# A second staging set for expert weights, with loads, squares and sums a stage apart

## The chip, the cores and the metric

The kernel runs on one core of a Trainium2 chip. Its engines are TensorE (PE, and PEld for its weight loads), VectorE (DVE), ScalarE (ACT), GpSimd (POOL) and SyncE (SP), which here only issues DMAs. The metric is the device time of one execution in microseconds; lower is better.

## What is computed

Three blocks follow each other:

```python
# 1. attention in chunks of 64 tokens, 4 x 8 heads, 576 tokens, head size 64
attn = softmax(q_c @ k_c.T / 8); x = attn @ v_c          # x: 2304 x 512
# 2. mixture of 8 experts, each token to its best one
e = argmax(x @ w_gate); gate_w = softmax(x @ w_gate)[e]
h = relu(disp[e] @ w1[e])                                # w1[e]: 512 x 1024
out[i] = gate_w[i] * (h @ w2[e])                         # w2[e]: 1024 x 512
# 3. feed-forward
hh = out @ w_in; y = (hh * sigmoid(hh)) @ w_out          # w_in: 512 x 2048
```

The capacity of an expert is 576 tokens. The weights of the feed-forward come as 64-bit floats.

## The kernel before

Matrix products are done in pairs of 16-bit numbers: a matrix is scaled by a power of two, rounded to 16 bits (the high half), and the remainder is the low half; three products of halves make one product. The scale of a weight matrix comes from the sum of its squares.

The expert phase has one stage for each expert e. In a stage the kernel runs `moe_tile(e, 0)`, then `more(e, 1)`: nested `If`s that run further tiles j = 1, 2, ... while the expert has more than 128 j tokens. A tile is 128 tokens: gathered from `x_d` (`gather`, GpSimd), transposed by a DMA (`t_dma`, SP), multiplied by w1 (L845), passed through Relu (`hh` on ScalarE, the low half `hl` on VectorE), multiplied by w2 (L866), scaled, split and scattered to `y_d` (GpSimd). The two halves of the first layer have a PSUM tile each.

Beside this the stage prepares the weights of the next experts. Weights of one expert are 8 pieces of 512 KB, 4 of w1 (m = 0) and 4 of w2 (m = 1). `w_prep(e, m, ...)` returns five steps: `sq(c)` squares piece c on ScalarE and sums each partition, `red` adds over partitions on TensorE (`total`, L124), `sc` reads that on VectorE and makes the scale, `hi(c)` makes the high half on GpSimd, `lo(c)` the low half on VectorE. The pieces lie in `st_s`, one set of 8; when `lo(c)` of expert e + 1 has read a piece, `lo_ld` issues the load of the same piece of expert e + 2 into its place, on SP's queue. Also in the stage, two chunks of `w_in` are converted from 64 bits by three VectorE operations each (`cb`) and squared on ScalarE (`cn`, L808).

The order on every engine is written out by hand. `slots[0]` to `slots[4]` hold what is issued at five places of `moe_tile(e, 0)`: before the first half, after it, after the second half, the same place again, and at three quarters of the second layer. `arms[j]` has the same for tile j inside the `If`. For j = 1 the `Else` arm runs `arms[0]`; for greater j it runs what is left of `arms[j]` and after. Each engine works through its own instructions in this order, and SP issues its DMAs in it.

In the stage of e the kernel before squares w2 of e + 1 (slots 1 and 2), sums and scales it (slot 4), makes the halves of e + 1, and, in `arms[1]` or the `Else` arm, squares, sums and scales w1 of e + 2, which has been loaded in the same stage. `win` and `wot` are regions for the converted weights of the feed-forward; in the expert phase conversions write `win` alone, and `wot` (17 rows of 512 floats in each partition) is first written after it.

In the profiled execution the 20 tiles are, by expert, 4, 1, 4, 3, 2, 1, 3 and 2.

Of the kernel before, what the change touches and what calls it, by code (L numbers as in the profile page):

```python
# [22 lines left out]
def attention_moe_ffn_kernel(  # L23
# [15 lines left out]
    nc = tc.nc  # L39
    B, H, S, D = q.shape  # L40
    NT, DM = out.shape
    E = w_gate.shape[1]
# [24 lines left out]
    st_s = [[(stage0, stage)[m].tile([P, 1024], F32, name=f"st{m}{c}") for c in range(4)] for m in range(2)]  # L67
# [32 lines left out]
    def pow2(n2, s, inv, kf, e2):  # L100
        n2i = n2.bitcast(I32)
        nc.vector.tensor_scalar(e2, n2i, 24, None, ALU.logical_shift_right)
        nc.vector.tensor_scalar(s.bitcast(I32), e2, -EXP1, kf * EXP1, ALU.mult, ALU.add)
        nc.vector.tensor_scalar(inv.bitcast(I32), e2, EXP1, (254 - kf) * EXP1, ALU.mult, ALU.add)  # L104
# [15 lines left out]
    def sums(m, n):  # L120
        return sum_at[-1][:, 16 * m:16 * m + n]

    def total(m, part):
        nc.tensor.matmul(out=sums(m, part.shape[-1]), lhsT=ones32, rhs=part)  # L124
# [3 lines left out]
    w_sp = {}  # L128
    w_fac = {}

    def w_piece(e, m, c):
        t = st_s[m][c]
        if m == 0:
            nc.sync.dma_start(out=t, in_=w1[e, c * P:(c + 1) * P, :])
        else:
            nc.sync.dma_start(
                out=t.rearrange("p (k f) -> p k f", k=2),
                in_=w2[e, 2 * c * P:(2 * c + 2) * P, :].rearrange("(k p) f -> p k f", p=P),
            )

    def w_load(e, m):
        for c in range(4):
            w_piece(e, m, c)

    def w_prep(e, m, hi_eng, lo_eng):
        st = st_s[m]
        sp = []
        n2 = wsm.tile([P, 4], F32, tag=f"n2{m}", name="n2", bufs=2)
        t2 = wsm.tile([P, 1], F32, tag=f"t2{m}", name="t2", bufs=2)
        e2 = wsm.tile([P, 1], I32, tag=f"e2{m}", name="e2", bufs=2)  # L150
        s = wsm.tile([P, 1], F32, tag=f"s{m}", name="s")
        inv = wsm.tile([P, 1], F32, tag=f"i{m}", name="inv")
        w_sp[e, m] = sp
        w_fac[e, m] = inv

        def sq(c):
            nc.scalar.activation(out=junk, in_=st[c], func=ACTF.Square, accum_out=n2[:, c:c + 1])  # L157

        def red():
            total(m, n2)  # L160

        def sc():
            nc.vector.tensor_reduce(out=t2, in_=sums(m, 4), axis=AX, op=ALU.add)
            pow2(t2, s, inv, KW, e2)

        def hi(c, hi_eng=hi_eng):
            if c == 0:
                sp.extend(ring.tile([P, 2, 1024], F16, tag=f"w{m}{i}", name="wsp") for i in range(4))
            if hi_eng is nc.scalar:
                nc.scalar.activation(out=sp[c][:, 0, :], in_=st[c], func=ACTF.Copy, scale=s)  # L170
            else:
                hi_eng.tensor_scalar(sp[c][:, 0, :], st[c], s, 1.0, ALU.mult, ALU.mult)  # L172

        def lo(c):
            lo_eng.scalar_tensor_tensor(  # L175
                out=sp[c][:, 1, :], in0=st[c], scalar=s, in1=sp[c][:, 0, :], op0=ALU.mult, op1=ALU.subtract
            )

        return sq, red, sc, hi, lo
# [116 lines left out]
    part = acc_p.tile([P, 1], F32, name="part")  # L296
# [276 lines left out]
    for t in range(-3, NTILE):  # L573
# [19 lines left out]
        u, i = divmod(t + 3, 2)  # L593
# [41 lines left out]
    prep = {(1, m): w_prep(1, m, nc.gpsimd, nc.vector) for m in range(2)}  # L635
# [29 lines left out]
    r = NBT - 1  # L665
# [43 lines left out]
    reg_p = tc_pool("reg", 1, reuse_waits="tile")  # L709
    win = reg_p.tile([P, KFF + 1, 512], F32, name="win")  # L710
    wot = reg_p.tile([P, KFF + 1, 512], F32, name="wot")
    fn2 = reg_p.tile([P, 2, KFF], F32, name="fn2")
    ft2 = reg_p.tile([P, 2], F32, name="ft2")
    fe2 = reg_p.tile([P, 2], I32, name="fe2")
# [175 lines left out]
    def g_next(e, j):  # L890
        gather(e, j, tabs[:, 0, e, j:j + 1])
# [89 lines left out]
    for e in range(E):  # L981
        last = e + 1 == E
        ops = [f_conv(c) for c in conv_of[e]]
        cb, cn = [lambda o=o: [f() for f in o[0:3]] for o in ops], [o[3] for o in ops]
        slots = [[], [], [], [], []]
        if not last:
            _, _, _, hi1, lo1 = prep[e + 1, 0]
            sq2, red2, sc2, hi2, lo2 = prep[e + 1, 1]

            def lo_ld(m, c):  # L990
                (lo1, lo2)[m](c)
                if e + 2 < E:
                    w_piece(e + 2, m, c)

            l1s, l2s = [[lambda m=m, c=c: lo_ld(m, c) for c in range(4)] for m in range(2)]
            g2 = lambda: g_next(e, 2)
            slots[0] = [lambda: g_next(e + 1, 0), *[lambda c=c: hi1(c) for c in range(4)]] if e else []
            slots[1] = [l1s[0], lambda: sq2(0), lambda: sq2(1)]
            slots[2] = [lambda: sq2(2), lambda: sq2(3), l1s[1], l1s[2], l1s[3]]
            slots[3] = [*([g2] if e else []), lambda: g_next(e + 1, 1)]  # L1000
            slots[4] = [red2, sc2, *[lambda c=c: hi2(c) for c in range(4)]]
        else:
            sp = [lambda c=c: f_split(0, c) for c in range(NSP)]
            slots = [[*cb, *cn], [], [], [], [lambda: f_red(0), lambda: f_sc(0), *sp]]

        def nxt0(k):
            if k < 0:
                if 0 < e < E - 1:
                    t_dma(e, 1)
            elif k == 0:  # L1010
                t_f1(e, 1)
                if last:
                    g_next(e, 2)
                else:
                    t_dma(e + 1, 0)
            elif not last:
                t_f1(e + 1, 0)
            else:
                with tc.If(n_e[e] <= SPLIT0):
                    y0_fac()  # L1020

        if e + 2 < E:
            for m in range(2):
                prep[e + 2, m] = w_prep(e + 2, m, nc.gpsimd, nc.vector)
        moe_tile(e, 0, *cols(e, 0), nxt0, lambda k: [f() for f in slots[k]])

        arms = {j: [[], [], [], [], []] for j in range(NJ)}
        if not last:
            sqs, red, sc = [], [], []
            if e + 2 < E:  # L1030
                sq, r, c1, _, _ = prep[e + 2, 0]
                sqs, red, sc = [lambda c=c: sq(c) for c in range(4)], [r], [c1]
            arms[0] = [*l2s, *sqs, *red, *cb, *cn, *sc]
            arms[1] = [l2s[0:1], [l2s[1], *sqs[0:2]], [*l2s[2:4], *sqs[2:4], cb[0], cn[0]], [], [*red, *sc]]
            arms[2] = [[], cb[1:2], [*cb[2:], *cn[1:]], [], []]
        else:
            arms[0] = []
        more(e, 1, arms)
        if e + 2 == E:
            t_dma(E - 1, 1)  # L1040
            with tc.If(n_e[E - 1] <= SPLIT0):
                y0_load()
# [122 lines left out]
    while conv:  # L1165
        step, left = [], left + 1.5
        c = NSP + len(bg)
# [29 lines left out]
    for s in range(len(seq) + LAG):  # L1197
        if s < len(seq):
            b, f = seq[s]
# [10 lines left out]
        if s >= LAG:  # L1210
            b, f = seq[s - LAG]
# [43 lines left out]
```

## Time and profile before

| what | value |
|---|---|
| median of 3 runs | 853.31 us (850.73 to 855.67) |
| profiled execution, its own time | 850.38 us |
| its span, first to last instruction | 848.6 us |
| busy: PE, PEld | 722.5 us (85%), 440.5 us (52%) |
| busy: DVE, ACT, POOL | 448.1, 333.2, 359.4 us |
| mean granted TensorE clock | 0.929 of full speed |
| weight pieces of the experts | 64 DMAs of 512 KB, 6.4 us to landing (median) |

Busy time is an average over phases with different limits. Attention lasts to about 150 us, the experts from there to 437 us, and the feed-forward to the end.

### The profile page before, as it was taken

The page shows a single profiled execution, that of the slowest core. Times are in us where ns is not written, and L with a number is a line of the kernel's source. Part 1 is how long each engine was busy: PE and PEld are TensorE (multiplying, and loading weights), DVE is VectorE, ACT ScalarE, POOL GpSimd, SP SyncE. Part 2 cuts the span into 40 slices and gives each one's busy share as a digit, 9 for nine tenths or more (in the row PEclk, how much of TensorE's full clock was granted, in tenths as well). Part 3 has the DMA queues.
Part 4 walks back from the last instruction along what each step waited for, and adds up shares of the span by engine and source line. Part 5 has one row for each costly group of instructions (what it writes and reads, how often), then busy time and mean ns, then how long its engine had stood idle before and what let it go on. Part 6 is the DMA issues. An engine that isn't in the chain of part 4 may idle for free.

```text
span 848.6 us, 14692 instructions
## 1 busy us (share of the span) xinstructions
PE 722.5 (85%) x5526; PEld 440.5 (52%) x5526; DVE 448.1 (53%) x920; ACT 333.2 (39%) x615; POOL 359.4 (42%) x355
## 2 busy tenths in 40 slices
PE   4798764998489989569798776999999999999995
PEld 3677654765456756447553333444444444565442
DVE  4365886654794758678339999633322223222000
ACT  5586737443443536442134455322232223223010
POOL 3475632524571737665167535544223223212111
PEclk9797955899699999979899999999999999999999
DMA  7988983992986798895635235020001000001000
GB/s 170 230 231 206 191 239 59 306 273 56 303 246 162 177 235 239 241 237 123 135 72 102 73 125 124 1 51 1 1 37 38 1 1 37 14 1 39 13 37 38
DMA packets 133325, 103.20 MB, mean 122 GB/s; under 512 B 85472, under 2 KB 112096, under 8 KB 133216
## 3 DMA queue, kind: packets, MB, share of 16 engines
q1 hardware_dynamic: 126784, 83.41, 40.2%
q0 software_dynamic: 5760, 18.39, 7.3%
q8 instruction: 60, 0.98, 0.5%
q14 instruction: 49, 0.40, 0.2%
q10 hardware_dynamic: 672, 0.02, 0.0%
HBM read 73.45 MB, written 14.71 MB: 104 GB/s over the span
## 4 chain that ended last, share of the span: by engine, by line
PE 30%; DVE 8%; issue 7%; DMA 4%; POOL 2%; ACT 1%; POOLq 0%; ACTq 0%; DVEq 0%
PE ops L1143 14%; PE fh L1115 14%; DMA out_dram<-ob,yrow 3%; DVE g L1126 2%; DVE th L1121 2%; DVE wot L797 1%; DVE wot L802 1%; PE mh L845 1%; DVE wot L794 1%; DVE win L734 1%; DMA y_d<-yr,tabs 1%; PE myp L866 0%; POOL win L751 0%; POOL win L749 0%; POOL win L750 0%
## 5 line engine op out<-in xcount | busy, mean ns | idle before, releaser
L1143 PE MATMUL ops<-wot,gh 128*128 128x512 f16 x576 | 171.3, 379 | 0.0
L1115 PE MATMUL fh<-yT,win 128*128 128x512 f16 (+1 forms) x768 | 156.9, 355 | 7.0 <-DVE g L1126 7.0
L1130 POOL TENSOR_TENSOR gl<-g,gh 128x512 f16<-128x512 f32 (+1 forms) x80 | 91.9, 1151 | 163.8 <-ACT gh L1128 163.8
L1115 PEld LDWEIGHTS <-win 128*128 128x128 f16 x960 | 94.2, 98 | 118.1 <-issue 26.1
L845 PE MATMUL mh<-mxT,wsp 128*128 128x128 f16 x1920 | 125.6, 233 | 17.7 <-PEq L930 9.4
L845 PEld LDWEIGHTS <-wsp 128*128 128x128 f16 x1920 | 123.5, 106 | 24.1 <-issue 19.9
L1143 PE MATMUL ops<-wot,gl 128*128 128x512 f16 x288 | 109.2, 379 | 0.0
L1121 DVE TENSOR_TENSOR th<-fh,rb 128x512 f32<-128x512 f32 (+1 forms) x64 | 39.8, 622 | 130.7 <-PE fh L1115 130.7
L1122 ACT ACTIVATE th<-th,fi 128x512 f32<-128x512 f32 (+1 forms) x80 | 54.3, 679 | 133.8 <-DVE th L1121 132.9
L175 DVE SCALAR_TENSOR_TENSOR wsp<-st,s,wsp 128x1024 f16<-128x1024 f32 x64 | 99.6, 1591 | 6.0 <-POOL wsp L172 6.0
L866 PE MATMUL myp<-wsp,hh 128*128 128x512 f16 x320 | 96.5, 384 | 0.0
L1143 PEld LDWEIGHTS <-gh 128*128 128x128 f16 x576 | 56.4, 98 | 64.1
L172 POOL TENSOR_SCALAR wsp<-st,s 128x1024 f16<-128x1024 f32 x56 | 75.2, 1359 | 20.0 <-DVE inv L104 11.4
L1128 ACT CAST gh<-g 128x512 f16<-128x512 f32 (+1 forms) x80 | 45.9, 574 | 73.2 <-DVE g L1126 54.3
L157 ACT ACTIVATE junk<-st 128x1024 bf16<-128x1024 f32 x64 | 67.4, 1053 | 16.4 <-DMA st<-in_moe_w_dram 15.3
L1126 DVE TENSOR_TENSOR g<-fh,th 128x512 f32<-128x512 f32 (+1 forms) x80 | 50.7, 634 | 38.8 <-ACT th L1122 32.4
L866 PE MATMUL myp<-wsp,hl 128*128 128x512 f16 x160 | 61.6, 385 | 8.2 <-DVE hl L851 8.0
L819 POOL DMA_INDIRECT xg<-x_d,tabs x34 | 45.4, 1336 | 35.2 <-issue 9.5
L882 POOL DMA_INDIRECT y_d<-yr,tabs x20 | 23.5, 1175 | 79.3 <-DVE yr L879 36.8
L851 DVE SCALAR_TENSOR_TENSOR hl<-mh,hh 128x512 f16<-128x512 f32 x40 | 27.5, 687 | 48.3 <-ACT hh L850 48.3
L1115 PE MATMUL fh<-st,win 128*128 128x512 f16 x192 | 43.5, 379 | 10.6 <-DVE g L1126 9.3
L866 PEld LDWEIGHTS <-hh 128*128 128x128 f16 x320 | 30.7, 101 | 29.8 <-ACT hh L850 0.8
(194 smaller groups left out, 849.8 us busy)
## 6 DMA issues: line engine op xcount, KB each, us to landing
st<-in_moe_w_dram SPq DMA_DIRECT2D x64, 512.0 KB, 6.4
fs<-in_moe_w_in_dram SPq DMA_DIRECT2D x16, 512.0 KB, 7.0
fs<-in_moe_w_out_dram SPq DMA_DIRECT2D x16, 512.0 KB, 3.4
vbd<-in_v_dram SPq DMA_DIRECT2D x72, 64.0 KB, 3.4
x_d<-xr SPq DMA_DIRECT2D x9, 512.0 KB, 6.1
ku<-in_k_dram SPq DMA_DIRECT2D x6, 512.0 KB, 5.7
qu<-in_q_dram SPq DMA_DIRECT2D x6, 512.0 KB, 8.3
ku<-in_k_dram SPq DMA_DIRECT2D x2, 384.0 KB, 4.2
```

The lines of the kernel that those rows point to most:

```text
L157: nc.scalar.activation(out=junk, in_=st[c], func=ACTF.Square, accum_out=n2[:, c:c + 1])
L172: hi_eng.tensor_scalar(sp[c][:, 0, :], st[c], s, 1.0, ALU.mult, ALU.mult)
L175: lo_eng.scalar_tensor_tensor(out=sp[c][:, 1, :], in0=st[c], scalar=s, in1=sp[c][:, 0, :], op0=ALU.mult, op1=ALU.subtract)
L845: nc.tensor.matmul(out=ps[:, f4, :], lhsT=a[c][:, part, f0:f0 + P], rhs=xt[:, rc, :], start=(n == 0), stop=(n == 3 * KD - 1),)
L866: nc.tensor.matmul(out=yp, lhsT=lh[:, f % 4, :], rhs=b[f // 2][:, part, (f % 2) * DM:(f % 2 + 1) * DM], start=(n == 0), stop=(n == 3 * KF1 ...
L1115: nc.tensor.matmul(out=hp[:, 0:n], lhsT=wv[:, part, c, :], rhs=yT_t[b](rc, n), start=(i == 0), stop=(i == 3 * KD - 1),)
L1121: nc.vector.tensor_tensor(out=th[:, 0:n], in0=hp[:, 0:n], in1=rb_t[b][:, 0:n], op=ALU.mult)
L1122: nc.scalar.activation(out=th[:, 0:n], in_=th[:, 0:n], func=ACTF.Sigmoid, scale=fi[:, 0:1])
L1126: nc.vector.tensor_tensor(out=g[:, 0:n], in0=hp[:, 0:n], in1=th[:, 0:n], op=ALU.mult)
L1128: nc.scalar.copy(out=gh[:, 0:n], in_=g[:, 0:n])
L1130: nc.gpsimd.tensor_tensor(out=gl[:, 0:n], in0=g[:, 0:n], in1=gh[:, 0:n], op=ALU.subtract)
L1143: nc.tensor.matmul(out=o_t[b][t], lhsT=lh[:, t * P:(t + 1) * P], rhs=wv[:, part, :], start=(f == 0 and i == 0), stop=(f == KFF - 1 and i = ...
```

## The change

Experts 2, 4 and 6 get a staging set of their own, `st_2`, eight views of `wot`; the others keep `st_s`. `lo_ld` now loads the pieces of e + 3 in place of those of e + 1, and stage 0 loads expert 2 as well, by `w_load(2, 0)` in slot 2 and `w_load(2, 1)` in slot 4. In the stage of e, w1 of e + 2 is squared in slots 1 and 2, and w2 of e + 2 in `arms[1]` or the `Else` arm; in stage 0 all eight squares of expert 2 are there, while slots 1 and 2 keep those of w2 of expert 1. Sum and scale of w1 of e + 1 stand in slot 0 of the next stage, ahead of its high halves; those of w2 stay in slot 4. No sum stands in an `Else` arm, and there the squares come after the conversions and their norms.

```diff
--- before.py
+++ after.py
@@ -128,8 +128,15 @@
     w_sp = {}
     w_fac = {}
 
+    st_2 = [[], []]
+
+    def st_of(e, m):
+        return st_2[m] if e >= 2 and e % 2 == 0 else st_s[m]
+
     def w_piece(e, m, c):
-        t = st_s[m][c]
+        if e >= E:
+            return
+        t = st_of(e, m)[c]
         if m == 0:
             nc.sync.dma_start(out=t, in_=w1[e, c * P:(c + 1) * P, :])
         else:
@@ -143,7 +150,7 @@
             w_piece(e, m, c)
 
     def w_prep(e, m, hi_eng, lo_eng):
-        st = st_s[m]
+        st = st_of(e, m)
         sp = []
         n2 = wsm.tile([P, 4], F32, tag=f"n2{m}", name="n2", bufs=2)
         t2 = wsm.tile([P, 1], F32, tag=f"t2{m}", name="t2", bufs=2)
@@ -709,6 +716,8 @@
     reg_p = tc_pool("reg", 1, reuse_waits="tile")
     win = reg_p.tile([P, KFF + 1, 512], F32, name="win")
     wot = reg_p.tile([P, KFF + 1, 512], F32, name="wot")
+    for i in range(8):
+        st_2[i // 4].append(wot[:, 2 * i:2 * i + 2, :].rearrange("p a b -> p (a b)"))
     fn2 = reg_p.tile([P, 2, KFF], F32, name="fn2")
     ft2 = reg_p.tile([P, 2], F32, name="ft2")
     fe2 = reg_p.tile([P, 2], I32, name="fe2")
@@ -983,22 +992,35 @@
         ops = [f_conv(c) for c in conv_of[e]]
         cb, cn = [lambda o=o: [f() for f in o[0:3]] for o in ops], [o[3] for o in ops]
         slots = [[], [], [], [], []]
+        if e + 2 < E:
+            for m in range(2):
+                prep[e + 2, m] = w_prep(e + 2, m, nc.gpsimd, nc.vector)
+
+        def part(x, m, i):
+            return [lambda c=c: prep[x, m][i](c) for c in range(4)] if x < E else []
+
         if not last:
-            _, _, _, hi1, lo1 = prep[e + 1, 0]
-            sq2, red2, sc2, hi2, lo2 = prep[e + 1, 1]
+            sqa, sqb = part(e + 2, 0, 0), part(e + 2, 1, 0)
 
             def lo_ld(m, c):
-                (lo1, lo2)[m](c)
-                if e + 2 < E:
-                    w_piece(e + 2, m, c)
+                prep[e + 1, m][4](c)
+                w_piece(e + 3, m, c)
 
             l1s, l2s = [[lambda m=m, c=c: lo_ld(m, c) for c in range(4)] for m in range(2)]
-            g2 = lambda: g_next(e, 2)
-            slots[0] = [lambda: g_next(e + 1, 0), *[lambda c=c: hi1(c) for c in range(4)]] if e else []
-            slots[1] = [l1s[0], lambda: sq2(0), lambda: sq2(1)]
-            slots[2] = [lambda: sq2(2), lambda: sq2(3), l1s[1], l1s[2], l1s[3]]
-            slots[3] = [*([g2] if e else []), lambda: g_next(e + 1, 1)]
-            slots[4] = [red2, sc2, *[lambda c=c: hi2(c) for c in range(4)]]
+            g2, gn = lambda: g_next(e, 2), lambda: g_next(e + 1, 1)
+            red2 = [*prep[e + 1, 1][1:3], *part(e + 1, 1, 3)]
+            if e == 0:
+                sq2 = part(1, 1, 0)
+                slots = [
+                    [], [l1s[0], *sq2[0:2]], [*sq2[2:4], *l1s[1:4], lambda: w_load(2, 0)], [gn],
+                    [*red2, lambda: w_load(2, 1)],
+                ]
+                sqb = [*sqa, *sqb]
+            else:
+                slots = [
+                    [lambda: g_next(e + 1, 0), *prep[e + 1, 0][1:3], *part(e + 1, 0, 3)], [l1s[0], *sqa[0:2]],
+                    [*sqa[2:4], *l1s[1:4]], [g2, gn], red2,
+                ]
         else:
             sp = [lambda c=c: f_split(0, c) for c in range(NSP)]
             slots = [[*cb, *cn], [], [], [], [lambda: f_red(0), lambda: f_sc(0), *sp]]
@@ -1019,19 +1041,12 @@
                 with tc.If(n_e[e] <= SPLIT0):
                     y0_fac()
 
-        if e + 2 < E:
-            for m in range(2):
-                prep[e + 2, m] = w_prep(e + 2, m, nc.gpsimd, nc.vector)
         moe_tile(e, 0, *cols(e, 0), nxt0, lambda k: [f() for f in slots[k]])
 
         arms = {j: [[], [], [], [], []] for j in range(NJ)}
         if not last:
-            sqs, red, sc = [], [], []
-            if e + 2 < E:
-                sq, r, c1, _, _ = prep[e + 2, 0]
-                sqs, red, sc = [lambda c=c: sq(c) for c in range(4)], [r], [c1]
-            arms[0] = [*l2s, *sqs, *red, *cb, *cn, *sc]
-            arms[1] = [l2s[0:1], [l2s[1], *sqs[0:2]], [*l2s[2:4], *sqs[2:4], cb[0], cn[0]], [], [*red, *sc]]
+            arms[0] = [*l2s, *cb, *cn, *sqb]
+            arms[1] = [l2s[0:1], [l2s[1], *sqb[0:2]], [*l2s[2:4], *sqb[2:], cb[0], cn[0]], [], []]
             arms[2] = [[], cb[1:2], [*cb[2:], *cn[1:]], [], []]
         else:
             arms[0] = []
```

## Rows read from the trace of the kernel before

**Rows 1.** Stretch; busy PE, PEld, DVE, ACT, POOL; granted clock, DMA share, GB/s
```profile
150.00:182.00 32.00, 29.45 (x313) 22.85 (x314) 20.11 (x45) 15.09 (x29) 16.21 (x14) 0.86 1.05 315
...
200.00:226.00 26.00, 11.47 (x125) 8.25 (x126) 20.88 (x30) 12.13 (x24) 18.02 (x13) 0.82 0.71 192
```

**Rows 2.** Whom TensorE waits for, 150 to 440 us: total, times, longest
```profile
PE fh L124 <- ACT junk L157: 12.6, 4, 9.9
PE fh L124 <- DVE win L797: 11.6, 1, 11.6
```

**Rows 3.** TensorE in order of time: start, us, what, idle before
```profile
225.55 0.56 PE L124 MATMUL fh<-n,ones 128*128 128x4 f32 x2 [11.59 <-DVE win L797]
225.97 7.63 PE L845 MATMUL mh<-mxT,wsp 128*128 128x128 f16 x96
...
241.00 5.52 PE L845 MATMUL mh<-mxT,wsp 128*128 128x128 f16 x96
...
253.17 5.52 PE L845 MATMUL mh<-mxT,wsp 128*128 128x128 f16 x96
...
263.71 1.50 PE L845 MATMUL mh<-mxT,wsp 128*128 128x128 f16 x24
```

**Rows 4.** The same, at the second hole
```profile
365.66 0.56 PE L124 MATMUL fh<-n,ones 128*128 128x4 f32 x2 [9.86 <-ACT junk L157]
```

**Rows 5.** SP's queue in order of time, first stage
```profile
163.50 1.56 SPq L134 DMA_DIRECT2D st<-in_moe_w_dram  x3
165.28 2.26 SPq L830 DMA_TRANSPOSE mxT<-xg  x1
```

**Rows 6.** Landing of the transpose issued at 165.28, then of 186.96
```profile
DMA to landing us min/median/max: 9.3/9.3/9.3
...
DMA to landing us min/median/max: 3.1/3.1/3.1
```

**Rows 7.** TensorE in the first expert's stage
```profile
177.19 6.50 PE L845 MATMUL mh<-mxT,wsp 128*128 128x128 f16 x96
...
200.01 5.53 PE L845 MATMUL mh<-mxT,wsp 128*128 128x128 f16 x96 [0.60 <-PEq L930]
```

**Rows 8.** DMA rate in 40 slices of 150 to 200 us
```profile
GB/s 256 216 328 408 390 387 194 305 358 173 267 386 379 129 365 416 429 205 59 353 387 399 348 311 399 349 298 358 54 329 144 122 0 0 112 112 0 13 0 0
```

**Rows 9.** ScalarE in order of time, tile 1 of expert 0
```profile
169.79 1.06 ACT L157 ACTIVATE junk<-st 128x1024 bf16<-128x1024 f32 x1 [1.22 <-DMA st<-in_moe_w_dram]
...
170.84 0.58 ACT L850 ACTIVATE hh<-mh 128x512 f16<-128x512 f32 x1
...
173.77 1.06 ACT L157 ACTIVATE junk<-st 128x1024 bf16<-128x1024 f32 x1 [1.32 <-DMA st<-in_moe_w_dram]
```

**Rows 10.** GpSimd in order of time, after expert 1
```profile
222.36 1.86 POOL L882 DMA_INDIRECT y_d<-yr,tabs  x1 [0.17 <-issue]
231.55 0.99 POOL L819 DMA_INDIRECT xg<-x_d,tabs  x1 [7.33 <-PE mh L845]
232.56 4.40 POOL L172 TENSOR_SCALAR wsp<-st,s 128x1024 f16<-128x1024 f32 x4
```

**Rows 11.** ScalarE there
```profile
228.14 0.63 ACT L808 ACTIVATE win<-win 128x512 f32<-128x512 f32 x1 [1.13 <-DVE t L163]
...
231.01 0.60 ACT L850 ACTIVATE hh<-mh 128x512 f16<-128x512 f32 x1 [2.15 <-issue]
231.50 1.05 ACT L157 ACTIVATE junk<-st 128x1024 bf16<-128x1024 f32 x1
232.45 0.19 ACT L157 ACTIVATION_READ_ACCUMULATOR junk<-st 128x1 f32 x1
```

**Rows 12.** VectorE there
```profile
233.74 4.30 DVE L175 SCALAR_TENSOR_TENSOR wsp<-st,s,wsp 128x1024 f16<-128x1024 f32 x1 [1.42 <-POOL wsp L172]
237.96 0.68 DVE L851 SCALAR_TENSOR_TENSOR hl<-mh,hh 128x512 f16<-128x512 f32 x1
```

**Rows 13.** Landing of the scatter issued at 222.36
```profile
DMA to landing us min/median/max: 7.7/7.7/7.7
```

## What the change is expected to do

> **What bounds the kernel now.** First the busy time by stretch, to see which engine is full where. From 150 to 182 us, the first expert's stage, the DMA engines are full (share 1.05, 315 GB/s); in the second expert's stage, 200 to 226 us, TensorE works 11.5 of 26 us and VectorE 20.9 [rows 1]. Then who TensorE waits for in the expert phase: two entries, 12.6 and 11.6 us, are of the sum at L124, and the row behind each is a square on ScalarE or the conversion that VectorE does meanwhile [rows 2]. Then TensorE in order of time. A tile that waits for nothing takes 10.5 us (253.17 to 263.71). The two large holes are at 225.55 (11.59 us) and 365.66 (9.86 us) [rows 3, 4], each where an expert has one tile only: its Else arm makes TensorE wait for four squares of weights that have hardly landed. The expert phase lasts to 437 us of 848.6 and the rest follows it, so a microsecond saved or lost there is one of the span unless something else says so.
>
> The reader is to see two kinds of stages: short ones (experts 1 and 5, one tile), with holes, and a long one (expert 0, four tiles) in which nothing waits for weights and the DMA queue has room only after its first loads.
>
> **Stage 0, where eight loads are added.** Before, this stage loads expert 2's eight pieces. After, it loads expert 3's eight, in the same places, and expert 2's eight besides: four at slot 2, four at slot 4 of tile 0. All sixteen are issued by SP, in program order, so the eight new ones stand ahead of the transpose t_dma(0,2) that tile 2 needs; behind it in turn come expert 3's second four, one f_load and t_dma(0,3). Before, the transpose is issued at 165.28 right behind the pieces of 163.50 to 165.06 [rows 5] and lands 9.3 us later, at 174.6; one with no load ahead of it lands in 3.1 us [rows 6]. So a transpose waits out what stands ahead of it in the queue. Tile 2 begins at 177.19 [rows 7], 2.6 us after.
>
> A piece is 0.524 MB. What it takes: at 315 GB/s [rows 1] 1.66 us; at the best slices, 429 GB/s [rows 8], 1.22; from the squares that wait for landings at 169.79 and 173.77, two pieces apart [rows 9], 1.99. I take 1.45, between the first two, because the squares' spacing includes gathers and a transpose. Eight pieces are 11.6 us (bounds 9.8 and 15.9): t_dma(0,2) lands at 186.2. Tile 2 starts 9.0 us late. TensorE has then stood idle. Where it does, its granted clock falls toward the lower of its two levels (1.2 of 2.4 GHz; mean 0.82 from 200 to 226 us [rows 1]): the tile after the hole at 225.55 needs 7.63 us for its first matmuls [rows 3], tile 2 here 6.50 [rows 7], so 1.1 more. **+10.1 us.** Tile 3 follows: its transpose stands behind five more loads, 186.2 + 5 x 1.45 + about 1 = 194.5, and tile 2 ends after that, near 199.
>
> The squares in the same tile give a second path. ScalarE now takes six squares of expert 2 in tile 1's slot 2 and two in slot 1, between the Relus of the halves. The first two land 2.9 us after the piece of 173.77, so both are squared by 177.9, and the second Relu, at 170.84 before [rows 9], comes 7 us later. Second-layer work covers some of it: tile 1 ends at about 181.6 instead of 177.19, **+4.4**. This is less than the transpose, hidden under it, and what is left if the transpose is not late.
>
> **Stages 2, 3 and 4, tile 1.** Before, the squares in this tile wait for pieces issued moments earlier, and the sum on TensorE waits for them. After, the data landed a stage ago and the sum is moved to the next stage's start. Expert 2's tile 1 takes 12.1 us (241.00 to 253.17), 1.6 over a free tile [rows 3]. For three stages the bounds are 0 and 4.8; I take **-2.5**. The sum itself, two small matmuls of 0.56 us [rows 3], is issued as often as before; at the stage's start its squares are a tile old. The scale that follows it on VectorE, and so the first high halves on GpSimd behind it, cost nothing: GpSimd first has the scatter and a gather to do, and reaches the high halves at 232.56, 6.6 us into the stage of 225.97 [rows 3, 10]. Without that cover the sum, the reduction and three small operations would be about 1 us of each stage.
>
> **Experts 1 and 5, where the holes are.** The sum leaves the Else arm, so TensorE goes on to the next expert's first layer. But it needs the Relu of ScalarE next, and that stands in a queue. The Else arm now runs low halves, conversions, norms, then four squares of w2: the squares come behind the norms, which wait for VectorE's conversions. The last norm starts at 228.14, and one square is 1.05 + 0.19 us [rows 11]. Norm done 228.9, four squares 233.9, Relu done 234.5; before, it ran at 231.01 [rows 11]. The Relu is 2.9 us later although TensorE is earlier. The second half's hl decides: it follows the first low half on VectorE, which took 4.30 us (233.74 to 238.04) because GpSimd's high halves ran from 232.56 to 236.96 [rows 10, 12]. GpSimd in turn resumed at its join when its scatter of 222.36 had landed, 7.7 us later [rows 13], whatever TensorE did. After: the low half ends at about 236.96 + 1.3 = 238.3, hl at 238.9, against 237.96 + 0.68 before. **0 us** for expert 1 (bounds: -4.5, were the Relu at 229 and GpSimd freed with it; +2, if TensorE, now idle in front of its second layer instead of its first, runs that at the lower clock). For expert 5, no weights are loaded any more in that stage, so the scatter lands sooner (at most by 7.7 - 3.1, the transposes' best, = 4.6); I take **-1**, bounds -4.5 and +2.
>
> The Trainium skill speaks the other way ("Trainium Kernel Development and Optimization", section Best Practices): double-buffer early, so that DMA overlaps compute. By that rule the two waits of [rows 2] simply go, 24.2 us, and the kernel would come to 853.3 - 24.2 = 829. The trace agrees that these waits exist; no row of it shows TensorE free to go on without them, since the Relu that it needs next is queued behind the same work.
>
> **Sum.** 10.1 - 2.5 + 0 - 1 = +6.6 us on the profiled execution: 850.4 to 857.0. The median of the runs shown is 2.9 above that execution, so the time is 853.3 + 6.6 = 859.9, given as 860.
>
> **Rivals.**
> (A) The forecast: the transpose behind eight loads decides, the holes only change their cause. 860.
> (B) The holes do close. ScalarE and GpSimd get through the join early, each hole gives 5 us (the 7.33 us that GpSimd stood before its gather [rows 10], less what VectorE still has to do): 860 + 1 - 10 = 851, no change. For it: GpSimd's and SP's waits at the join may have hung on TensorE's late sum. Against it: the landing of the scatter and VectorE's 20.9 us of work.
> (C) Not slower, one mechanism: the transposes get through beside the loads. It decides at 181.6 us: a t_dma(0,2) landed by then, when tile 1 ends, costs nothing, and stage 0 loses only 4.4 to the squares. 860 - 10.1 + 4.4 = 854, no change. For it: the queue runs on 16 engines; against it: 9.3 us behind loads and 3.1 without [rows 6].
> (D) Faster: stage 0 absorbs the loads and the holes close, 860 - 10.1 - 9 = 841, and 829 at the far end, if nothing takes the place of either wait. For it: the DMA engines have room at the end of stage 0 (0 to 144 GB/s in its last ten slices [rows 8]), so the bytes fit into the stage as a whole; against it: the place in SP's order. The double-buffering rule of the Trainium skill is this rival at its far end.
>
> Chances: A 0.63, B 0.12, C 0.13, D 0.12. A's own range is 856 to 868: up by 4.3 if a piece takes 1.99, and by 4 for two cold second layers; down by 1.8 for a piece at 1.22 and by 2.3 for all of the tile 1 gain. The range that leaves out no more than 2 in 10 reaches to B: 849 to 868.
>
> A measurement of this kernel tells 0.5%, 4.3 us, from no change. Slower by more: A without its lowest edge and a little of C, 0.63. Faster by more: D and some of B, 0.16. The same: 0.21.
>
> **What would show it.** In the profile after: t_dma(0,2) landing near 186 and the third tile of stage 0 starting there, at 180 or before if wrong; squares of expert 2 that wait for DMA in tile 1, none in later stages; no sum in the holes after experts 1 and 5, but a wait of the second layer for hh at the same place, with four squares ahead of the Relu on ScalarE; expert 2's tile 1 under 11 us. The prediction is wrong if tile 2 starts on time, or if expert 1's tile and expert 2's first together take over 3 us less than the 41.0 us from 200.01 to 241.00 [rows 3, 7].

## The result, and the profile after

The changed kernel takes 861.84 us (median of four runs, 859.77 to 865.17) against 852.02 us (four runs, 850.35 to 855.67) before: a ratio of 1.0113, 95% interval 1.0065 to 1.0162. It is slower, by 9.8 us by the medians; the forecast was 860, or 6.6 more than before. The profiled execution took 861.44 us with a span of 859.6 us, so it is 11.0 longer than that of before.

First, where the 11.0 us are. Stages are cut at the first `mh` matmul of each expert, the phase of the experts at the first matmul of the feed-forward. The third row is another profile of the kernel before, taken for the experiments below.

| profile | experts begin | experts last | rest | stage of expert 0 | 1 + 2 | 3 | 4 | 5 + 6 | 7 |
|---|---|---|---|---|---|---|---|---|---|
| before | 150.8 | 286.3 | 411.6 | 49.2 | 75.1 | 40.1 | 28.4 | 65.8 | 27.7 |
| after | 154.7 | 293.4 | 411.5 | 60.5 | 72.7 | 37.3 | 29.4 | 65.8 | 27.7 |
| before, again | 155.9 | 284.8 | 411.5 | 44.9 | 75.8 | 41.4 | 26.7 | 68.4 | 27.7 |

Of the 11.0 us, 3.9 lie ahead of the experts, where the change touches nothing, and they are there in the second profile of before too. In the expert phase it is +7.1 against the one profile of before and +8.6 against the other; the forecast was +6.6. All of the loss is in the first stage: +11.3 us against the one profile of before, +15.6 against the other, while the later stages together are 4.2 and 7.0 us shorter.

TensorE in order of time, as in [rows 3, 4, 7] (start, us, what, idle before it and what ended that):

```profile
154.72 7.16 PE L854 MATMUL mh<-mxT,wsp 128*128 128x128 f16 x96 [2.06 <-DMA mxT<-xg]
...
167.03 5.52 PE L854 MATMUL mh<-mxT,wsp 128*128 128x128 f16 x96
184.63 1.04 PE L875 MATMUL myp<-wsp,hh 128*128 128x512 f16 x2 [9.49 <-ACT hh L859]
191.77 5.52 PE L854 MATMUL mh<-mxT,wsp 128*128 128x128 f16 x96 [1.83 <-DMA mxT<-xg]
202.30 5.52 PE L854 MATMUL mh<-mxT,wsp 128*128 128x128 f16 x96
...
230.95 0.45 PE L124 MATMUL fh<-n,ones 128*128 128x4 f32 x2 [3.39 <-PEq L939]
231.33 0.37 PE L854 MATMUL mh<-mxT,wsp 128*128 128x128 f16 x2
236.34 7.78 PE L854 MATMUL mh<-mxT,wsp 128*128 128x128 f16 x94 [4.63 <-issue]
247.53 0.61 PE L875 MATMUL myp<-wsp,hh 128*128 128x512 f16 x2 [3.42 <-ACT hh L859]
...
254.76 5.52 PE L854 MATMUL mh<-mxT,wsp 128*128 128x128 f16 x96
265.39 4.80 PE L854 MATMUL mh<-mxT,wsp 128*128 128x128 f16 x83
...
387.87 1.04 PE L875 MATMUL myp<-wsp,hh 128*128 128x512 f16 x2 [10.17 <-POOL wsp L179]
```

The first four rows are the loss: expert 0's tile 1 lasts from 167.03 to 191.77, 24.7 us instead of 13.6, held first for 9.49 us by a Relu and then for 1.83 by the transpose of tile 2. The long waits of the sum (11.59 and 9.86 us, [rows 3, 4]) are gone; at the same places the second layer now waits (3.42 and 10.17 us). Expert 2's tile 1 is a free tile: 254.76 to 265.39, 10.6 us.

ScalarE in expert 0's tile 1, where [rows 9] were, and after expert 1, where [rows 11] were:

```profile
169.91 0.60 ACT L859 ACTIVATE hh<-mh 128x512 f16<-128x512 f32 x1 [0.83 <-PE mh L854]
181.57 1.06 ACT L164 ACTIVATE junk<-wot 128x1024 bf16<-128x1024 f32 x1 [11.06 <-DMA wot<-in_moe_w_dram]
...
182.94 1.06 ACT L164 ACTIVATE junk<-wot 128x1024 bf16<-128x1024 f32 x1 [0.23 <-DMA wot<-in_moe_w_dram]
...
184.00 0.58 ACT L859 ACTIVATE hh<-mh 128x512 f16<-128x512 f32 x1
...
190.90 1.06 ACT L164 ACTIVATE junk<-wot 128x1024 bf16<-128x1024 f32 x1 [0.19 <-DMA wot<-in_moe_w_dram]
...
242.31 1.04 ACT L164 ACTIVATE junk<-st 128x1024 bf16<-128x1024 f32 x1
...
246.90 0.58 ACT L859 ACTIVATE hh<-mh 128x512 f16<-128x512 f32 x1
```

The second Relu of tile 1 stands behind two squares of expert 2, whose first piece lands at 181.57. The eight pieces follow each other until 190.90. After expert 1, four squares from 242.31 stand ahead of the Relu at 246.90, as forecast.

SP's queue in order of time, and the landing of the transpose issued at 181.62 (before: [rows 5, 6]):

```profile
169.51 3.23 SPq L141 DMA_DIRECT2D wot<-in_moe_w_dram  x4
173.53 5.60 SPq L143 DMA_DIRECT2D wot<-in_moe_w_dram  x4
181.62 3.90 SPq L839 DMA_TRANSPOSE mxT<-xg  x1
...
DMA to landing us min/median/max: 10.1/10.1/10.1
```

The eight new loads stand ahead of t_dma(0,2), which lands at 191.7; tile 2 starts then. Counted from the start of the experts, the landing is 13.2 us later than before (37.0 instead of 23.8), and 12.4 of these lie ahead of the issue (26.9 instead of 14.5): SP issues the eight loads from 169.51 to 179.13 and then stands 2.5 us. From issue to landing it is 10.1 us instead of 9.3, so most of the delay does not show in the time to landing.

### The profile page after: what moved, and what is told of

It reads as the page before. It is cut to its first block, busy times and chain, and to the rows that moved or that the text cites. A ratio compares the mean times of both kernels' runs of the same rounds, so it can differ in the third digit from the quotient of the medians.

```text
span 859.6 us, 14673 instructions
## 1 busy us (share of the span) xinstructions
PE 719.0 (84%) x5526; PEld 435.1 (51%) x5526; DVE 448.0 (52%) x920; ACT 333.1 (39%) x615; POOL 360.5 (42%) x355
## 5 line engine op out<-in xcount | busy, mean ns | idle before, releaser
L854 PE MATMUL mh<-mxT,wsp 128*128 128x128 f16 x1920 | 121.8, 229 | 16.6 <-issue 8.4
L854 PEld LDWEIGHTS <-wsp 128*128 128x128 f16 x1920 | 119.9, 104 | 21.4 <-issue 16.6
L875 PE MATMUL myp<-wsp,hh 128*128 128x512 f16 x320 | 99.5, 394 | 23.1 <-ACT hh L859 12.9
L1141 DVE TENSOR_TENSOR g<-fh,th 128x512 f32<-128x512 f32 (+1 forms) x80 | 50.7, 634 | 38.7 <-ACT th L1137 33.3
L891 POOL DMA_INDIRECT y_d<-yr,tabs x20 | 25.9, 1296 | 86.4 <-DVE yr L888 35.4
L828 POOL DMA_INDIRECT xg<-x_d,tabs x34 | 44.0, 1294 | 35.8 <-DMA xg<-x_d,tabs 9.4
L182 DVE SCALAR_TENSOR_TENSOR wsp<-st,s,wsp 128x1024 f16<-128x1024 f32 x40 | 56.8, 1450 | 0.0
L1130 PE MATMUL fh<-st,win 128*128 128x512 f16 x192 | 43.5, 379 | 10.7 <-DVE g L1141 9.1
L179 POOL TENSOR_SCALAR wsp<-st,s 128x1024 f16<-128x1024 f32 x32 | 43.2, 1366 | 12.7 <-DVE inv L104 7.8
L1158 PEld LDWEIGHTS <-gl 128*128 128x128 f16 x288 | 28.2, 98 | 34.0
```

Source lines behind the costliest of these rows:

```text
L182: lo_eng.scalar_tensor_tensor(out=sp[c][:, 1, :], in0=st[c], scalar=s, in1=sp[c][:, 0, :], op0=ALU.mult, op1=ALU.subtract)
L828: nc.gpsimd.indirect_dma_start(out=t, out_offset=None, in_=x_d[:, :], in_offset=bass.IndirectOffsetOnAxis(ap=idx, axis=0))
L854: nc.tensor.matmul(out=ps[:, f4, :], lhsT=a[c][:, part, f0:f0 + P], rhs=xt[:, rc, :], start=(n == 0), stop=(n == 3 * KD - 1),)
L875: nc.tensor.matmul(out=yp, lhsT=lh[:, f % 4, :], rhs=b[f // 2][:, part, (f % 2) * DM:(f % 2 + 1) * DM], start=(n == 0), stop=(n == 3 * KF1 ...
L1130: nc.tensor.matmul(out=hp[:, 0:n], lhsT=wv[:, part, c, :], rhs=yT_t[b](rc, n), start=(i == 0), stop=(i == 3 * KD - 1),)
L1141: nc.vector.tensor_tensor(out=g[:, 0:n], in0=hp[:, 0:n], in1=th[:, 0:n], op=ALU.mult)
```

## Experiments

All but sum_only and control_before start from the changed kernel. Ratios are to runs of the kernel before on the same chip. The first four runs take stage 0 apart.

| run | ratio to before, 95% | experts last | stage 0 | expert 1 + tile 0 of 2 | tile 1 of 2 |
|---|---|---|---|---|---|
| the change | 1.0113 (1.0065 to 1.0162) | 293.4 | 60.5 | 39.5 | 10.6 |
| tdma_first | 1.0066 (1.0041 to 1.0092) | 293.5 | 59.5 | 40.2 | 10.8 |
| sq_late | 1.0092 (1.0060 to 1.0124) | 300.5 | 63.4 | 39.7 | 10.8 |
| tdma_and_sq | 1.0090 (1.0067 to 1.0114) | 296.1 | 64.3 | 40.3 | 10.5 |
| e2_first | 0.9958 (0.9931 to 0.9985) | 284.8 | 51.1 | 39.1 | 10.7 |
| sum_only | 1.0021 (0.9988 to 1.0053) | 286.7 | 47.3 | 41.7 | 10.5 |
| else_sq | 1.0157 (1.0115 to 1.0199) | 297.7 | 60.7 | 42.0 | 11.2 |
| lo_after_hl | 1.0073 (1.0019 to 1.0128) | 292.8 | 61.9 | 39.4 | 10.5 |
| else_sq_lo | 1.0076 (1.0034 to 1.0118) | 294.2 | 61.2 | 32.7 | 18.8 |
| hi_act | 1.0029 (1.0002 to 1.0056) | 292.9 | 60.4 | 33.7 | 12.7 |
| best | 0.9925 (0.9890 to 0.9960) | 279.2 | 50.0 | 35.6 | 16.4 |
| best_hi | 0.9925 (0.9898 to 0.9953) | 286.0 | 50.7 | 37.9 | 12.2 |
| control_before | 0.9981 (0.9952 to 1.0009) | 284.8 | 44.9 | 42.8 | 11.0 |

**tdma_first: the transpose of expert 0's tile 2 ahead of the loads.**

```diff
-                if k < 0 and j + 1 < NJ:
+                if k < 0 and j + 1 < NJ and (e, j) != (0, 1):
                     t_dma(e, j + 1)
...
                     t_dma(e + 1, 0)
+                if e == 0:
+                    t_dma(0, 2)
```

> The changed kernel with one transpose moved: t_dma(0,2) is issued in tile 0, ahead of the eight added loads. Theory (two things hold stage 0 at about the same time, the squares of expert 2 ahead of the second Relu of tile 1 and the transpose behind the loads): the squares still hold tile 1, so tile 2 starts when tile 1 ends, 1.8 us sooner than in the changed kernel; about 860 us. Rival (the transpose alone holds): 9 us less, 853.

TensorE in order of time:

```profile
167.18 5.53 PE L854 MATMUL mh<-mxT,wsp 128*128 128x128 f16 x96
185.07 1.03 PE L875 MATMUL myp<-wsp,hh 128*128 128x512 f16 x2 [9.78 <-ACT hh L859]
190.13 5.52 PE L854 MATMUL mh<-mxT,wsp 128*128 128x128 f16 x96
```

Tile 2 no longer waits for its transpose, but tile 1 is only 1.7 us shorter (23.0 instead of 24.7): the Relu behind the squares holds it alone.

**sq_late: the squares out of tile 1, the transpose left where it is.**

```diff
+            if e == 0:
+                arms[1] = [l2s[0:1], [l2s[1]], [*l2s[2:4], cb[0], cn[0]], [], []]
+                arms[2] = [[], cb[1:2], [*cb[2:], *cn[1:], *sqb[0:4]], [], []]
+                arms[3] = [[], [], sqb[4:8], [], []]
```

> The changed kernel with the eight squares of expert 2 moved from tile 1 of stage 0 to tiles 2 and 3; the loads and the transpose stay. Theory: tile 1 is free again, but t_dma(0,2) lands as late as before, so tile 2 starts at most 2 us sooner; about 861 us. Rival (the squares alone hold stage 0): 9 us less, 853.

TensorE at tile 2:

```profile
192.13 8.25 PE L854 MATMUL mh<-mxT,wsp 128*128 128x128 f16 x96 [15.31 <-DMA mxT<-xg]
```

The Relu is free, and the transpose takes its place: one wait of 15.31 us, after which the first layer takes 8.25 us instead of 5.52. Each of the two waits is thus enough for the whole loss.

**tdma_and_sq: both edits together.**

> Both edits together. Theory: tile 2 starts about 10 us sooner than in the changed kernel, but t_dma(0,3) now holds, since it still stands behind thirteen loads and lands some 197 us into the span; tile 3 starts there instead of 202, so only 3 to 5 us are won: about 858 us. Rival (nothing else in stage 0 waits for the queue): 9 to 10 us less, 852.

TensorE at tile 3, and below it, from its own view, the landing of the transpose that it waited for:

```profile
177.08 5.52 PE L854 MATMUL mh<-mxT,wsp 128*128 128x128 f16 x96
203.24 8.07 PE L854 MATMUL mh<-mxT,wsp 128*128 128x128 f16 x96 [15.46 <-DMA mxT<-xg]
```

```profile
DMA to landing us min/median/max: 12.8/12.8/12.8
```

A gain of 3 to 5 us was expected and none came: the ratio is that of the change within the intervals, and stage 0 takes 64.3 us. Tiles 1 and 2 take 10.5 and 26.2: the transpose of tile 3, issued at 190.38, lands 12.8 us later. As long as sixteen loads are issued in tiles 0 and 1, a transpose stands behind them, whichever it is.

**e2_first: expert 2's pieces in the places of expert 1's, expert 3's eight a tile later.**

```diff
-                w_piece(e + 3, m, c)
+                w_piece(e + 3 if e else 2, m, c)
...
-                    [], [l1s[0], *sq2[0:2]], [*sq2[2:4], *l1s[1:4], lambda: w_load(2, 0)], [gn],
-                    [*red2, lambda: w_load(2, 1)],
+                    [], [l1s[0], *sq2[0:2]], [*sq2[2:4], *l1s[1:4]], [gn],
+                    red2,
...
+            if e == 0:
+                late = [lambda: w_load(3, 0), lambda: w_load(3, 1)]
+                arms[0] = [*l2s, *late, *cb, *cn, *sqb]
+                arms[1] = [l2s[0:1], [l2s[1], *sqb[0:2]], [*l2s[2:4], *sqb[2:4], cb[0], cn[0]], [], []]
+                arms[2] = [late, cb[1:2], [*cb[2:], *cn[1:], *sqb[4:8]], [], []]
```

> The changed kernel with another order of the loads in stage 0: expert 2's eight go where expert 3's were, and expert 3's eight are issued in tile 2, behind t_dma(0,3). Squares of expert 2: four in tile 1, four in tile 2. Same loads, squares and bytes, later stages unchanged. Theory (the place in SP's order costs, not the bytes): stage 0 falls from 60.5 to 47 to 49 us, 850 us in all. Rival (the bytes themselves do it, or the loss lies elsewhere): no more than 4 us won, 858 or over.

TensorE at tiles 2 and 3 and at the end of the stage:

```profile
176.84 5.52 PE L854 MATMUL mh<-mxT,wsp 128*128 128x128 f16 x96
189.19 5.52 PE L854 MATMUL mh<-mxT,wsp 128*128 128x128 f16 x96 [1.64 <-DMA mxT<-xg]
205.01 0.56 PE L124 MATMUL fh<-n,ones 128*128 128x4 f32 x2 [5.11 <-PEq L939]
```

The same number of loads, half of them in tile 2 instead of tiles 0 and 1. Tiles 0 to 2 take 10.7, 11.8 and 12.4 us, the stage 51.1 us, 9.4 less but not the 47 to 49 of the theory, and the whole is 0.4% faster than before. A new wait of 5.11 us at the branch ahead of expert 1 is part of what is left. So the loss lies in when the loads are issued, not in their number. The edit also moves four squares of expert 2 into tile 2, but sq_late, which moves squares alone, gains nothing.

The next four runs are about the two holes, after experts 1 and 5.

**sum_only: the kernel before, its sum of w1 moved into the next stage, loads and squares as before.**

```diff
-            slots[0] = [lambda: g_next(e + 1, 0), *[lambda c=c: hi1(c) for c in range(4)]] if e else []
+            slots[0] = [lambda: g_next(e + 1, 0), *prep[e + 1, 0][1:3], *[lambda c=c: hi1(c) for c in range(4)]] if e else []
...
-            arms[0] = [*l2s, *sqs, *red, *cb, *cn, *sc]
-            arms[1] = [l2s[0:1], [l2s[1], *sqs[0:2]], [*l2s[2:4], *sqs[2:4], cb[0], cn[0]], [], [*red, *sc]]
+            arms[0] = [*l2s, *sqs, *cb, *cn]
+            arms[1] = [l2s[0:1], [l2s[1], *sqs[0:2]], [*l2s[2:4], *sqs[2:4], cb[0], cn[0]], [], []]
```

> The kernel before with one part of the change alone: the sum and scale of w1 of e + 1 leave arms[1] and the Else arm and stand in slot 0 of the next stage, ahead of the high halves. Loads and squares stay. Theory: the waits at the sum (11.6 and 9.9 us) go, but GpSimd's chain still sets hl after experts 1 and 5: expert 1 and expert 2's first tile 40 to 41 us as before (41.0), the waits in tile 1 of stages 0, 2 and 3 go: 2 to 4 us less than the kernel before in all. Rival (the late sum holds everything behind it): 5 us less at each of the two places and the 2 to 4 besides, 12 to 14 less.

Whom TensorE waits for, 150 to 450 us (total, times, longest):

```profile
PE fh L124 <- ACT junk L157: 11.9, 1, 11.9
...
PE fh L124 <- DVE wsp L175: 8.0, 1, 8.0
PE fh L124 <- ACT win L808: 6.5, 1, 6.5
```

The sum waits as long in its new place (11.9 us against 11.59), and the time is that of before. So the move alone does not take these waits off the sum; the change also has the loads a stage earlier. The loads without the move were not run.

**else_sq: in Else arms the squares ahead of conversions and norms.**

```diff
-            arms[0] = [*l2s, *cb, *cn, *sqb]
+            arms[0] = [*l2s, *sqb, *cb, *cn]
```

> The changed kernel with the four squares in the Else arms put ahead of the conversions and norms. Theory (after experts 1 and 5 the second half's hl decides, and it stands behind a VectorE low half that waits for GpSimd, which resumes when its scatter has landed): the Relu after expert 1 comes 4 us sooner, the end of expert 2's first tile does not; expert 1 and expert 2's first tile together 39 to 40 us as in the changed kernel (39.5), expert 5 and expert 6's first 39.5 to 40.5 (40.4); the whole 0 to -1.5 us against the changed kernel. Rival (the Relu behind the squares is what holds): 3 to 4 us less at both places, 7 in all.

VectorE, then TensorE:

```profile
248.40 4.30 DVE L182 SCALAR_TENSOR_TENSOR wsp<-st,s,wsp 128x1024 f16<-128x1024 f32 x1 [4.20 <-POOL wsp L179]
252.62 0.68 DVE L860 SCALAR_TENSOR_TENSOR hl<-mh,hh 128x512 f16<-128x512 f32 x1
```

```profile
253.36 0.61 PE L875 MATMUL myp<-wsp,hl 128*128 128x512 f16 x1 [5.38 <-DVE hl L860]
```

The Relu's wait goes, and TensorE waits 5.38 us for `hl` instead. It stands behind the low half, which waits for GpSimd's high half. This chain is the one that the forecast put at this place. The two tiles take 42.0 us, neither the 39 to 40 of the theory nor the 36 of the rival; 2.5 us more than in the change is within what two profiles of one kernel differ by (see control_before).

**lo_after_hl: the first low half of a stage behind both Relus and their low halves.**

```diff
-                    [lambda: g_next(e + 1, 0), *prep[e + 1, 0][1:3], *part(e + 1, 0, 3)], [l1s[0], *sqa[0:2]],
-                    [*sqa[2:4], *l1s[1:4]], [g2, gn], red2,
+                    [lambda: g_next(e + 1, 0), *prep[e + 1, 0][1:3], *part(e + 1, 0, 3)], [*sqa[0:2]],
+                    [*sqa[2:4], *l1s[0:4]], [g2, gn], red2,
```

> The changed kernel with the first low half of w1 (and the load behind it) moved from slot 1 to slot 2 in the stages of experts 1 to 6, so that the second half's hl no longer stands behind it on VectorE. Theory: the waits of the second layer for hl, 4.0 us over three tiles in the changed kernel, go; after experts 1 and 5 nothing changes, since there the Relu behind the squares is now as late as hl; 3 to 4 us less in all. Rival (hl alone holds after experts 1 and 5): 2 to 4 us more at each of the two places, 8 to 12 in all.

TensorE, after experts 1 and 5:

```profile
247.69 1.03 PE L875 MATMUL myp<-wsp,hh 128*128 128x512 f16 x2 [5.81 <-ACT hh L859]
...
387.04 1.04 PE L875 MATMUL myp<-wsp,hh 128*128 128x512 f16 x2 [12.81 <-ACT hh L859]
```

39.4 us at the first hole against 39.5: nothing, as the theory has it. The 3 to 4 us that it expects elsewhere can't be seen: the expert phase is 0.6 us shorter. The Relu behind the Else arm's squares still holds TensorE, 5.81 us after expert 1 and 12.81 us after expert 5.

**else_sq_lo: both of these.**

> Both edits together. Theory: two chains end at the same place after experts 1 and 5, the Relu behind the squares and hl behind the low half, so both have to go: 4 us less at each of the two places (36 us each), 11 to 12 us less in all than the changed kernel. Rival (either edit alone does it, or the scatter's landing holds whatever stands on VectorE and ScalarE): no more than the better of the two single edits.

ScalarE and VectorE, behind the first hole, then TensorE:

```profile
257.67 0.69 ACT L886 ACTIVATE yr<-myp,ys 128x512 f16<-128x512 f32 x1 [6.83 <-DVE yinv L104]
```

```profile
248.56 7.88 DVE L182 SCALAR_TENSOR_TENSOR wsp<-st,s,wsp 128x1024 f16<-128x1024 f32 x4 [0.79 <-POOL wsp L179]
```

```profile
234.81 7.72 PE L854 MATMUL mh<-mxT,wsp 128*128 128x128 f16 x94 [4.03 <-issue]
244.22 0.60 PE L875 MATMUL myp<-wsp,hh 128*128 128x512 f16 x2 [1.69 <-ACT hh L859]
...
258.89 0.61 PE L875 MATMUL myp<-wsp,hh 128*128 128x512 f16 x2 [3.42 <-ACT hh L859]
```

Now the hole closes: 32.7 us instead of 39.5. But the next tile takes 18.8 us instead of 10.6 and gives it all back. The four low halves, which pace themselves by GpSimd's high halves (7.88 us), have tile 0's scaling behind them, ScalarE waits 6.83 us for that, and tile 1's Relu stands behind ScalarE.

**control_before: the kernel before, profiled again.**

> The kernel before, once more, with a profile of its own. The first expert matmul starts at 150.8 us in the one profile of before and at 154 to 156.5 in those of the changed kernels, one of which (sum_only) stages its loads as before does. Theory: those 4 us vary from run to run; this profile starts the experts anywhere from 150 to 156, the expert phase takes 286 +/- 2 us, the ratio is 1.000 within 0.5%. Rival: the changed code shifts the attention; then this profile starts the experts at 150.8 +/- 0.5 again.

TensorE at the first matmuls of experts 0 and 1:

```profile
155.94 6.96 PE L845 MATMUL mh<-mxT,wsp 128*128 128x128 f16 x96 [3.81 <-DMA mxT<-xg]
...
200.80 5.53 PE L845 MATMUL mh<-mxT,wsp 128*128 128x128 f16 x96 [0.59 <-PEq L930]
```

The experts begin at 155.94 us, so the 3.9 us ahead of them are no work of the change. Single stages of the same kernel differ by up to 4.7 us between its two profiles (stage 5: 22.5 and 27.2; stage 0: 49.2 and 44.9), the expert phase by 1.5. Terms of a microsecond or two can't be read from one pair of profiles.

**best: e2_first and else_sq_lo together.**

> e2_first (stage 0 in 51 us) and else_sq_lo (expert 1 and tile 0 of expert 2 in 33) together. Theory: GpSimd's chain after the join (landing of the scatter, gather, four high halves) stays as it is, so that expert 2's tile 1 takes 18 us again and what the two holes gain is given back; the expert phase takes 284 to 286 us, the median no less than e2_first's 852. Rival, the two gains add: 285 - 12 = 273, median near 841.

Neither theory's number: 279.2 us, median 849.05 against 857.16 before. Expert 2's tile 1 takes 16.4 us, as the theory has it, and the first hole with it 52.0 us against 49.8 in e2_first; the second gives 5.5 less than there (36.0 instead of 41.5). It is the fastest seen, with best_hi 0.75% under before, but its interval overlaps that of e2_first, so that it beats e2_first is not settled.

**hi_act: as else_sq_lo, with w1's high halves of experts 2 and later on ScalarE.**

```diff
-                prep[e + 2, m] = w_prep(e + 2, m, nc.gpsimd, nc.vector)
+                prep[e + 2, m] = w_prep(e + 2, m, (nc.scalar, nc.gpsimd)[m], nc.vector)
...
-                    [lambda: g_next(e + 1, 0), *prep[e + 1, 0][1:3], *part(e + 1, 0, 3)], [l1s[0], *sqa[0:2]],
-                    [*sqa[2:4], *l1s[1:4]], [g2, gn], red2,
+                    [lambda: g_next(e + 1, 0), *prep[e + 1, 0][1:3]], [*part(e + 1, 0, 3)[0:2]],
+                    [*part(e + 1, 0, 3)[2:4], *sqa, *l1s], [g2, gn], red2,
...
-            arms[0] = [*l2s, *cb, *cn, *sqb]
+            arms[0] = [*l2s, *sqb, *cb, *cn]
```

> As else_sq_lo, but the high halves of w1 of experts 2 and later are made on ScalarE instead of GpSimd. Theory: in else_sq_lo what stood behind GpSimd's chain was the low halves and with them VectorE and the second tile's Relu; taken off GpSimd, expert 1 with tiles 0 and 1 of expert 2 falls from 51.5 us to about 45 and the expert phase from 294 to about 286. Rival: VectorE's own work there (20.9 us of 26 in the second stage of before) is the bound; then the sum stays at 50 to 52 and the expert phase at 292 to 296.

VectorE, then TensorE further on:

```profile
247.69 4.86 DVE L182 SCALAR_TENSOR_TENSOR wsp<-st,s,wsp 128x1024 f16<-128x1024 f32 x4
```

```profile
307.19 0.39 PE L875 MATMUL myp<-wsp,hl 128*128 128x512 f16 x1 [1.84 <-DVE hl L860]
...
331.94 0.56 PE L124 MATMUL fh<-n,ones 128*128 128x4 f32 x2 [7.60 <-PEq L939]
```

The low halves take 4.86 us instead of 7.88, and expert 1 with tiles 0 and 1 of expert 2 comes to 33.7 + 12.7 = 46.4 us instead of 51.5, as the theory expected: here GpSimd's chain was the bound, not VectorE. (best_hi, below, does not repeat this.) The expert phase did not follow (292.9, not 286), because stage 3 takes 45.7 us instead of 37.3: its tile 1 takes 14.7 us instead of 10.8, behind the squares that ScalarE had no time for before, and the branch ahead of expert 4 takes 7.60 us instead of 1.9 to 6.3 in the runs above.

**best_hi: e2_first and hi_act together.**

> e2_first and hi_act together. Theory: the 9 us of stage 0 and the gain at the two holes add, so that the expert phase takes 272 to 280 us and the median is 840 to 848, below before. Rival: VectorE is the bound at the holes, and it comes out as e2_first, 285 and 852.

286.0 us, median 851.84 against 857.16: faster than before by 0.75%, no better than best, and not the 840 to 848 of the theory. The numbers are the rival's, 285 and 852, though not for its reason at both holes: after expert 5 the two tiles take 35.8 us instead of the 41.5 of e2_first. After expert 1 the three tiles take 50.1 us against 49.8 there, so that what hi_act gained is not seen again, and whether GpSimd or VectorE is the bound at that hole stays open. Stage 3 takes 44.9 us here too, with 7.00 us at its last branch. What makes that branch longer in these two kernels stays open; in sum_only it is 6.31.

## Why the prediction was right

**Stage 0, +10.1 forecast, +11.3 measured against the profile of before, +15.6 against the control.** The transpose behind eight loads was forecast to land 35.4 us after the experts begin (186.2 - 150.8); it landed after 37.0 (191.7 - 154.7), with a piece each 1.33 us (seven from 181.57 to 190.90) instead of 1.45. Tile 2 started 10.6 us late instead of 9.0, and right behind the landing. The 1.1 us for a cold first layer did not come: tile 2's took 5.52 us.

**The step that failed is the second path, the squares: +4.4, "hidden under it".** By itself it is as long as the first. Tile 1's last matmul ended near 189.9 (191.77 - 1.83), 35.2 us after the experts began, where the forecast had 30.8 (181.6 - 150.8): the term is +8.8. Half of the error is the Relu, which came 2.2 us later than forecast because the pieces landed later. The other half is the work behind it: TensorE came back from 9.49 us of waiting at half its rate (1.04 us for a pair that takes 0.59; granted clock 0.50 from 184.6 to 188.6, the level of 1.2 GHz). The forecast charged the cold clock to tile 2 and none to the rest of tile 1. Since both paths end within 2 us of each other, the sum did not show it, and that a term of 8.8 us still ended under the first is luck: nothing in the forecast kept it there. tdma_first did: without the first path 1.0 us of the stage comes back, where the forecast's numbers would give 5.7 (10.1 - 4.4).

**Rival C falls by the same row.** The transposes do not get through, and had they, 8.8 us rather than 4.4 would have stayed; tdma_first, which brings that about by hand, measures a ratio of 1.0066, where 854 us would be 1.001.

**The first hole, 0 forecast.** Expert 1 with expert 2's tile 0 takes 39.5 us against 41.0 and 42.8 in the two profiles of before: -1.5 to -3.3, inside the bounds. GpSimd, where [rows 10] were, and VectorE, where [rows 12] were:

```profile
235.91 1.86 POOL L891 DMA_INDIRECT y_d<-yr,tabs  x1 [0.16 <-issue]
245.16 0.99 POOL L828 DMA_INDIRECT xg<-x_d,tabs  x1 [7.40 <-DMA xg<-x_d,tabs]
246.18 4.41 POOL L179 TENSOR_SCALAR wsp<-st,s 128x1024 f16<-128x1024 f32 x4
...
384.62 1.00 POOL L828 DMA_INDIRECT xg<-x_d,tabs  x1 [6.50 <-DMA fs<-in_moe_w_in_dram]
```

```profile
247.51 0.69 DVE L860 SCALAR_TENSOR_TENSOR hl<-mh,hh 128x512 f16<-128x512 f32 x1 [5.40 <-ACT hh L859]
248.11 3.55 DVE L182 SCALAR_TENSOR_TENSOR wsp<-st,s,wsp 128x1024 f16<-128x1024 f32 x1
251.59 0.68 DVE L860 SCALAR_TENSOR_TENSOR hl<-mh,hh 128x512 f16<-128x512 f32 x1
```

Landing of the scatter issued at 235.91 (before: [rows 13]):

```profile
DMA to landing us min/median/max: 7.8/7.8/7.8
```

GpSimd stands 7.40 us as it stood 7.33, and the second `hl` at 251.59 stands behind the low half of 248.11, as forecast. The profiles bear out the forecast that GpSimd waits for its scatter, although the rows name another releaser (a matmul before, a gather after): in the twelve of the fourteen profiles that have this landing, it comes 7.7 to 8.8 us after the issue, and the gather starts 1.4 to 1.5 us behind it. But `hl` did not decide alone: TensorE waited 3.42 us for the Relu, and `hl`, done at 252.27, was then there 0.2 us before the matmul that needs it. Both queues, ScalarE's squares and this chain, had to go before the hole closed (else_sq and lo_after_hl alone gain nothing, else_sq_lo 6.8 us). Rival B is right that the hole can close, but its mechanism is not seen: in else_sq_lo GpSimd still stands 7.32 us, and two more edits were needed to take the path of TensorE out of its way.

**The second hole, -1 forecast, +0.8 and -1.2 measured.** The scatter's earlier landing did not help: it landed 4.3 us after its issue instead of 6.7, and yet GpSimd waits 6.50 us, by the profile until an f_load landed. The 10.17 us at 387.87 are put down to GpSimd's high halves; ScalarE's Relu there started at 387.24, so both end together.

**Tile 1 of experts 2 to 4, -2.5 forecast.** Against the profile of before, -1.6, -0.9 and -1.8; against the control (11.0, 11.8 and 13.6 us), -0.4, -1.0 and +0.7. The squares no longer wait for DMA after stage 0, as expected, but what that gives lies between -4.3 and -0.7. The forecast took one execution's 12.1 us for the kernel's.

**Rival D.** Its condition, stage 0 absorbing the loads, is what e2_first brings about, by issuing half of them a tile later. The Trainium skill ("Trainium Kernel Development and Optimization", section Best Practices) says to double-buffer for performance, and not how early. That agrees with e2_first, 0.4% faster. It does not agree with the far end of the rival, 829: at the holes the waits of the sum are replaced by those for the Relu and for GpSimd's chain.

## What to carry to other kernels

A load issued earlier stands ahead of every transfer issued after it: look up which small transfer of the current tile it now precedes, and issue the bulk behind it, spread over tiles. Two late paths may end together, so remove each alone and both before naming a cause, and count the cold clock on whatever work comes behind the wait. Where a wait has two queues behind it, an edit to one shows nothing, and a gain is to be looked for again in the next tile before it is believed.

## What the runs showed of the hardware

TensorE stands at branches, for which the forecast has no term. At the `If` ahead of expert 2 its sequencer stood 3.39 us (at 230.95) and then, two matmuls later, 4.63 us for nothing that the profile shows. Elsewhere its sequencer stood 0.6 to 7.6 us; ahead of expert 4 it was 3.62 and 4.99 in the two profiles of before. From 228 to 237 us the two queues of kind "instruction" carry two and four packets, 0.03 MB each, while the queue of the loads is at 87.1%. The Trainium skill ("Runtime: NRT & Kernel Launch", section Instruction fetch mechanics) says that a taken branch whose target is not at hand makes the sequencer fetch a page before it goes on. The rows agree with this and do not prove it. At this place it costs little: in the change and in else_sq_lo (4.03 us) a wait for the Relu follows it, 3.42 and 1.69 us, and that Relu stands behind other work of ScalarE. No run here removes a branch.

After sq_late's wait of 15.31 us the clock is low for nearly a whole first layer: 8.25 us instead of 5.52, granted clock 0.63 from 192 to 200 us, and 1.00 from 206 to 216.
